# Mixture-of-experts stage of an attention kernel: expert tiles of 128 slots instead of 256, three weight sets with guarded loads, and tiles past the 36th in conditional blocks

## The chip, the cores and the metric

The kernel runs on one core of one Trainium2 chip. The metric is device time in microseconds (us); lower is better. The engines are named as the profile names them: PE (TensorE, matmuls) with PEld (its weight loads), DVE (VectorE), ACT (ScalarE), POOL (GpSimd) and SP (SyncE, which here only issues DMAs).

## What is computed

Two stages in one program, all in float32. First a sliding-window causal attention (8 batches, 8 heads, 576 positions, head size 64, window 64). Its output, laid out as 4608 tokens of 512 numbers, feeds a mixture of experts in which every token goes to exactly one of 8 experts.

```python
scores = np.where((rel >= 0) & (rel < 64), q @ k.T / 8, -1e9)
attn = softmax(scores); x = (attn @ v) as (4608, 512)
logits = x @ w_gate                      # (4608, 8)
expert_idx = np.argmax(logits, axis=1)
gate_w = softmax(logits)[arange, expert_idx]
for e in range(8):                       # rows of x grouped by expert
    h = np.maximum(x_sorted[lo:hi] @ w1[e], 0.0)   # w1[e]: 512 x 1024
    y_sorted[lo:hi] = h @ w2[e]                    # w2[e]: 1024 x 512
out = gate_w[:, None] * y_in_token_order
```

The inputs are drawn with a fixed seed. With them the experts 0 to 7 get 669, 400, 748, 505, 592, 390, 566 and 738 tokens.

## The kernel before

The program has three stages.

Attention: for each of 8 batches and 4 head pairs the kernel transposes q and k on PE, makes the scores of three blocks of 64 queries at a time, adds a mask, exponentiates, and multiplies by v. Every two batches it makes the router logits (line 234, matmuls with 8 columns) and writes x to memory (`x_dram`). SP loads q, k and v of a batch while the one before is at work, in two sets of buffers.

Routing: the kernel ranks every token within its expert and gives it a slot. Slots are cut into tiles of TB = 256, each tile belonging to one expert; an expert's last tile may be partly empty. `tile_e` holds the expert of each tile. From the slots two tables are made by one-hot matmuls (`lo`, `hi`, `slots`, lines 385 to 400): `perm_i`, the token of each slot, and `gate_s`, its gate.

Experts (lines 428 to 470): there are NTILE = 18 + 7 = 25 tiles, enough for any routing, and all 25 are computed. `fetch(i)` has SP load both weight matrices of the tile's expert, 2 MB each, into one of two sets (`wp`, bufs=2), whatever the tile before used, and has POOL gather the 256 tokens by an indirect DMA in two halves of 128 rows (`xg`). For each tile PE then does

- 8 transposes of the gathered rows (line 437), copied to `xgT` by DVE and ACT,
- the first product `hp`, 8 groups of 4 matmuls with 256 columns (line 445), each group made positive and copied to `hT` by DVE or ACT,
- the second product `yp`, 2 halves of 8 matmuls with 512 columns (line 456), scaled by the gate and scattered to the output by an indirect DMA of POOL.

A float32 matmul that is not a transpose is two PE instructions, each with a weight load of its own, so a tile has 64 of the first kind and 32 of the second. A scheduler orders each engine's instructions by a model of their cost; buffers in pools make the waits.

```python
fetched = {0: fetch(0)}
for i in range(NTILE):
    if i + 1 < NTILE:
        fetched[i + 1] = fetch(i + 1)
    w1, w2, xg = fetched.pop(i)
```

Of the kernel before, what the change touches and what calls it, by code (L numbers as in the profile page):

```python
# [18 lines left out]
WINDOW = 64  # L19
# [15 lines left out]
def kernel(  # L35
# [18 lines left out]
    NG = H // 2              # head pairs: one pair fills the 128 partitions  # L54
    NB = S // WINDOW         # query blocks of one window; each sees itself and the block before
    GB = 3                   # query blocks handled together
    KB = (S + P - 1) // P    # row tiles of 128, the last one half full
    NV = NB // 2             # whole ones
    SM = NV * P
    BG = 2                   # batches that together fill whole token blocks  # L60
    NTB = BG * S // P        # token blocks in such a group
    NJ = NT // P             # token blocks in all
    FT = FF // P
    TB = 256                 # slots of one expert tile
    C = TB // P
    NTILE = (NT + TB - 1) // TB + E - 1   # enough for any routing
    NS = NTILE * C
# [7 lines left out]
    # x in token order, and after it one row of zeros for the slots without a token  # L75
# [8 lines left out]
    tile_e = consts.tile([P, NTILE], I32, name="tile_e")  # L84
    zrow = consts.tile([1, DM], F32, name="zrow")
    nc.vector.memset(zrow[:], 0.0)

# [1 line left out]
    with (  # L89
# [12 lines left out]
        # additive masks over [(head, query), key]: slot 0 for the first block, whose  # L102
        # keys are blocks 0 and 1; the others for the keys of the block before and its own
# [17 lines left out]
        # q transposed, each head of the pair in its own columns and zeros beside it  # L121
# [19 lines left out]
        def load_v(b):  # L141
# [5 lines left out]
            # the same keys half a tile later  # L147
# [137 lines left out]
    with (  # L285
# [12 lines left out]
        e_m = iota([P, E], [[1, E]], base=-E)                    # e - E  # L298
# [4 lines left out]
        tok_m = iota([P, NJ], [[P, NJ]], base=-NT, cm=1)         # token - NT, never 0  # L303
        before = rt.tile([P, P], F32, name="before")             # [p', p] = p' < p
# [6 lines left out]
        keep = rt.tile([P, E, NJ], F32, name="keep")             # 0 where a scan starts again  # L311
# [7 lines left out]
        # the first expert of the largest logit, and its probability  # L319
# [16 lines left out]
        # rank of a token among those of its expert: lower partitions of its column, columns before  # L336
# [14 lines left out]
        # tiles of each expert, up to and with it, and the slot where it starts  # L351
# [17 lines left out]
        V.tensor_copy(out=tile_e[:], in_=te[:])  # L369

# [13 lines left out]
        # the other way round: token and gate of every slot [slot % P, slot // P]  # L384
# [18 lines left out]
    w1v = moe_w1.rearrange("e (g p) f -> p e g f", p=P)  # L403
    w2v = moe_w2.rearrange("e (t p) d -> p e t d", p=P)
    with (
        tc.tile_pool(name="wp", bufs=2) as wp,
        tc.tile_pool(name="mp", bufs=2) as mp,
# [91 lines left out]
```

## Time and profile before

| | us |
|---|---|
| three runs | 1118.69, 1118.84, 1123.08 (median 1118.84) |
| span of the profiled execution | 1121.2 |
| attention, up to the last router logits | 333.8 |
| routing and first gathers | 51.4 |
| 25 expert tiles, first `hp` to last `yp` | 724.9 |
| after the last matmul | 11.1 |

| engine | busy us | share of the span |
|---|---|---|
| PE | 1031.5 | 92% |
| PEld | 753.1 | 67% |
| DVE | 350.9 | 31% |
| ACT | 277.1 | 25% |
| POOL | 211.8 | 19% |

The profile records one execution, with every instruction's start and duration by engine and by line, the DMA traffic, and the TensorE clock that was granted (1.00 is 2.4 GHz, 0.50 is 1.2 GHz). Times are counted from the span's start. Matmuls are pipelined: the duration of one is longer than the distance between two starts, so the cost of a stream of matmuls is read from starts. A row that says x20 merges 20 instructions that follow each other.

### The profile page before, as it was taken

The numbers are of one execution on the slowest core, as the hardware profiler recorded it, in microseconds if no ns is written. First come the engines' busy times: TensorE is split into PE (matmuls) and PEld (weight loads), VectorE is DVE, ScalarE is ACT, GpSimd is POOL, SyncE is SP. The second block draws the span as 40 slices with busy tenths as digits, with TensorE's granted clock in tenths as the row PEclk, the third lists the DMA queues.
The fourth block names the chain that finished last, engine by engine and source line by source line (L and its number), as shares of the span: only waits on it lengthen the run. The fifth ranks groups of instructions, "written<-read, shape, count | busy, mean of one in ns | idle before, by whom it ended". The sixth has DMA issues, their size and how long they took to land. (4 is left out here: it accounts for less than half of the span.)

```text
span 1121.2 us, 13320 instructions
## 1 busy us (share of the span) xinstructions
PE 1031.5 (92%) x4868; PEld 753.1 (67%) x4868; DVE 350.9 (31%) x949; ACT 277.1 (25%) x968; POOL 211.8 (19%) x243
## 2 busy tenths in 40 slices
PE   5999898988975699999999999999999999999996
PEld 4888887877864566666666666666666666666663
DVE  5887787877847010111111011111101111111010
ACT  3675675765730000100000000000000000000000
POOL 3442342333220400111111111111111111110000
PEclk9999999999975799999999999999999999999998
DMA  9873654762002774444444555554544445454400
GB/s 198 142 127 109 140 92 133 123 124 89 1 1 85 284 266 176 175 165 170 165 179 178 184 188 187 188 182 170 188 174 170 169 159 174 182 185 150 150 1 0
DMA packets 165491, 166.04 MB, mean 148 GB/s; under 512 B 116912, under 2 KB 116912, under 8 KB 165426
## 3 DMA queue, kind: packets, MB, share of 16 engines
q1 hardware_dynamic: 152242, 133.20, 40.9%
q0 software_dynamic: 8000, 22.56, 5.3%
q10 hardware_dynamic: 5184, 9.44, 2.2%
q8 instruction: 38, 0.62, 0.2%
q14 instruction: 27, 0.22, 0.1%
HBM read 146.29 MB, written 22.55 MB: 151 GB/s over the span
## 5 line engine op out<-in xcount | busy, mean ns | idle before, releaser
L445 PE MATMUL hp<-xgT,w 128*128 128x256 f32 x1600 | 352.3, 381 | 0.8 <-ACT xgT L438 0.8
L456 PE MATMUL yp<-w,hT 128*128 128x512 f32 x800 | 347.4, 592 | 0.0
L445 PEld LDWEIGHTS hp<-xgT,w 128*128 128x128 f32 x1600 | 303.1, 191 | 43.3 <-ACT xgT L438 1.0
L456 PEld LDWEIGHTS yp<-w,hT 128*128 128x128 f32 x800 | 152.0, 190 | 180.7 <-issue 179.4
L467 POOL DMA_INDIRECT out_dram<-y,perm_i x50 | 50.0, 1001 | 532.9 <-DVE y L465 492.1
L452 DVE TENSOR_SCALAR hT<-hp 128x256 f32<-128x256 f32 x100 | 42.5, 425 | 302.6 <-PE hp L445 302.6
L450 ACT ACTIVATE hT<-hp 128x256 f32<-128x256 f32 x100 | 38.4, 384 | 326.3 <-PE hp L445 245.3
L204 POOL TENSOR_TENSOR pr<-pr,sm 128x384 f32<-128x384 f32 x96 | 79.4, 828 | 206.2 <-DVE sm L203 68.9
L198 ACT ACTIVATE pr<-pr,mx 128x128 f32<-128x128 f32 x288 | 112.6, 392 | 21.5 <-DVE mx L195 18.7
L463 ACT ACTIVATE y<-yp,gate_s 128x512 f32<-128x512 f32 x25 | 17.2, 688 | 334.4 <-PE yp L456 334.4
L186 PE MATMUL sc<-kT,qd 128*128 128x128 f32 x576 | 90.5, 287 | 2.5 <-DVE pr L192 1.3
L465 DVE TENSOR_SCALAR y<-yp,gate_s 128x512 f32<-128x512 f32 x25 | 18.8, 751 | 202.2 <-PE yp L456 202.2
L186 PEld LDWEIGHTS sc<-kT,qd 128*128 128x128 f32 x576 | 75.8, 196 | 7.0 <-DVE pr L192 3.9
L421 POOL DMA_INDIRECT xg<-x_dram,perm_i x50 | 49.3, 986 | 157.2 <-PE tp L437 100.2
L210 PE MATMUL pt<-ident,pr 128*128 128x128 f32 x288 | 54.5, 292 | 19.1 <-POOL pr L204 17.5
L438 DVE COPY xgT<-tp 128x512 f32<-128x512 f32 x25 | 17.3, 692 | 150.7 <-PE tp L437 149.3
L217 PE MATMUL pv<-pT,va 128*128 128x128 f32 x320 | 61.4, 291 | 3.0 <-DVE pT L212 2.7
L192 DVE TENSOR_TENSOR pr<-sc,mask 128x384 f32<-128x384 f32 x96 | 52.7, 549 | 17.0 <-PE sc L186 14.8
L212 DVE COPY pT<-pt 128x384 f32<-128x384 f32 x96 | 52.6, 550 | 17.1 <-PE pt L210 16.2
L210 PEld LDWEIGHTS pt<-ident,pr 128*128 128x128 f32 x288 | 33.7, 147 | 30.4 <-POOL pr L204 29.4
L198 ACT ACTIVATION_READ_ACCUMULATOR pr<-pr,mx 128x1 f32 x288 | 53.9, 187 | 0.0
L217 PE MATMUL pv<-pT,vb 128*128 128x128 f32 x256 | 52.3, 288 | 0.6 <-ACT xT L224 0.3
(94 smaller groups left out, 760.7 us busy)
## 6 DMA issues: line engine op xcount, KB each, us to landing
w<-in_moe_w_dram SPq DMA_DIRECT2D x50, 2048.0 KB, 9.4
x_dram<-xs ACTq DMA_DIRECT2D x36, 256.0 KB, 2.0
qs<-in_q_dram SPq DMA_DIRECT2D x32, 256.0 KB, 5.0
ks<-in_k_dram SPq DMA_DIRECT2D x32, 256.0 KB, 5.1
va<-in_v_dram SPq DMA_DIRECT2D x32, 256.0 KB, 5.0
qs<-in_q_dram SPq DMA_DIRECT2D x8, 128.0 KB, 5.0
ks<-in_k_dram SPq DMA_DIRECT2D x8, 128.0 KB, 4.6
vb<-in_v_dram SPq DMA_DIRECT2D x8, 128.0 KB, 4.5
```

Of the source, the lines that this page charges most:

```text
L186: nc.tensor.matmul(sc[:, n, :], lhsT=qd[:, i].rearrange("d h s -> d (h s)"), rhs=kT[:, k0 : k0 + P], start=True, stop=True,)
L192: nc.vector.tensor_tensor(out=pr[:], in0=sc[:], in1=mask[:, m0 : m0 + GB, :], op=ALU.add)
L198: nc.scalar.activation(out=pr[:, n, :], in_=pr[:, n, :], func=AF.Exp, scale=scale, bias=mx[:, n : n + 1], accum_out=sm[:, n : n + 1],)
L204: nc.gpsimd.tensor_tensor(out=pr[:], in0=pr[:], in1=_inner(sm[:], P), op=ALU.mult)
L210: nc.tensor.transpose(out=pt[:, n, :], in_=pr[:, n, :], identity=ident[:])
L212: nc.vector.tensor_copy(out=pT[:], in_=pt[:])
L217: nc.tensor.matmul(pv[:, n, :], lhsT=vt[:, 2 * g : 2 * g + 2, :].rearrange("p h d -> p (h d)"), rhs=pT[:, n, :], start=True, stop=True,)
L421: nc.gpsimd.indirect_dma_start(out=t[:], out_offset=None, in_=x_dram[:, :], in_offset=bass.IndirectOffsetOnAxis(ap=perm_i[:, i * C + c : i ...
L445: nc.tensor.matmul(hp[:], lhsT=w1[:, 0, g, f * P : (f + 1) * P], rhs=xgT[:, g, :], start=(g == 0), stop=(g == NG - 1),)
L452: nc.vector.tensor_scalar_max(hT[:, f, :], hp[:], 0.0)
L456: nc.tensor.matmul(yp[:], lhsT=hT[:, f, c * P : (c + 1) * P], rhs=w2[:, 0, f, :], start=(f == 0), stop=(f == FT - 1),)
L467: nc.gpsimd.indirect_dma_start(out=out[:, :], out_offset=bass.IndirectOffsetOnAxis(ap=perm_i[:, s : s + 1], axis=0), in_=y[:], in_offset=N ...
```

## The change

A tile holds 128 slots. The most tiles any routing can need is now 36 + 7 = 43. With the token counts above, the experts need 6, 4, 6, 4, 5, 4, 5 and 6 tiles, 40 in all.

- A tile has one gather, 4 transposes (`turn`), a first product of 32 matmuls with 128 columns in two groups of 16 that each fill one PSUM tile and are copied by one instruction (DVE for the first, ACT for the second), a second product of 8 matmuls with 512 columns, one scaling on ACT and one scatter. The transposes of tile i+1 stand in the code between the two products of tile i.
- Tile i uses weight set i mod 3. `load_i` says for each tile whether its expert differs from that of the tile three before; the two weight DMAs of a tile are issued with that as a condition. Set 0 is filled with expert 0's weights during the attention stage (after the loads of the last batch in the code), and tile 0 reloads it only where its expert is not 0. Gathered rows have four buffers. SP keeps the order of the code in the expert stage.
- Tiles 0 to 35 always run. Every engine then reads the number of used tiles (`used`), and tiles 36 and up stand in four blocks of two (the last of one), each under a condition.
- In the routing stage the tables have 43 instead of 50 columns, the cuts 36 instead of 18, and `used_i` and `load_i` are made.

```diff
-    TB = 256                 # slots of one expert tile
-    C = TB // P
-    NTILE = (NT + TB - 1) // TB + E - 1   # enough for any routing
-    NS = NTILE * C
+    TB = P
+    NTILE = (NT + TB - 1) // TB + E - 1
+    NS = NTILE
+    NW = 3
...
+    load_i = consts.tile([P, NTILE], I32, name="load_i")
+    used_i = consts.tile([P, 1], I32, name="used_i")
...
+    ws = [weights(consts, 0)]
...
+                if b + 2 == B:
+                    nc.sync.dma_start(out=ws[0][0][:], in_=w1v[:, 0:1, :, :])
+                    nc.sync.dma_start(out=ws[0][1][:], in_=w2v[:, 0:1, :, :])
...
+        V.tensor_copy(out=used_i[:], in_=cum[:, E - 1 : E])
+
+        V.tensor_single_scalar(load_i[:, 0:1], te[:, 0:1], 0.0, op=ALU.not_equal)
+        V.memset(load_i[:, 1:NW], 1)
+        V.tensor_tensor(out=load_i[:, NW:], in0=te[:, NW:], in1=te[:, 0 : NTILE - NW], op=ALU.not_equal)
...
-        tc.tile_pool(name="wp", bufs=2) as wp,
+        tc.tile_pool(name="wp", bufs=1) as wp,
...
-        tc.tile_pool(name="ps_h", bufs=3, space=PSUM) as ps_h,
+        tc.tile_pool(name="ps_h", bufs=4, space=PSUM) as ps_h,
         tc.tile_pool(name="ps_y", bufs=2, space=PSUM) as ps_y,
+        tc.manual_schedule(engines={mybir.EngineType.SP}),
...
+        def fetch(i):
+            w1, w2 = ws[i % NW]
             e = nc.sync.value_load(tile_e[0:1, i : i + 1], min_val=0, max_val=E - 1)
...
+            new = nc.sync.value_load(load_i[0:1, i : i + 1], min_val=0, max_val=1)
+            nc.sync.dma_start(out=w1[:], in_=w1v[:, bass.ds(e, 1), :, :], cond=new, cond_hint=False)
+            nc.sync.dma_start(out=w2[:], in_=w2v[:, bass.ds(e, 1), :, :], cond=new, cond_hint=False)
+            nc.gpsimd.indirect_dma_start(
+                out=xgs[i % NX][:], out_offset=None, in_=x_dram[:, :],
+                in_offset=bass.IndirectOffsetOnAxis(ap=perm_i[:, i : i + 1], axis=0),
+            )
+
+        def turn(i):
+            tp = ps_xt.tile([P, NG, P], F32, name="tp")
+            for g in range(NG):
+                nc.tensor.transpose(out=tp[:, g, :], in_=xgs[i % NX][:, g * P : (g + 1) * P], identity=ident[:])
+            nc.vector.tensor_copy(out=xgTs[i % 2][:], in_=tp[:])
+
+        def work(i, ahead):
...
+            for m in range(2):
+                hp = ps_h.tile([P, HF, TB], F32, name="hp")
+                for f in range(HF):
+                    for g in range(NG):
+                        c0 = (m * HF + f) * P
+                        nc.tensor.matmul(
+                            hp[:, f, :], lhsT=w1[:, 0, g, c0 : c0 + P], rhs=xgT[:, g, :],
+                            start=(g == 0), stop=(g == NG - 1),
+                        )
+                if m:
+                    nc.scalar.activation(out=hT[:, m * HF :, :], in_=hp[:], func=AF.Relu)
+                else:
+                    nc.vector.tensor_scalar_max(hT[:, 0:HF, :], hp[:], 0.0)
+            if ahead:
+                turn(i + 1)
...
+        for i in range(NCUT):
+            fetch(i + AHEAD)
+            work(i, True)
+
+        used = nc.values_load(used_i[0:1, 0:1], min_val=NCUT, max_val=NTILE)
+        for i0 in range(NCUT, NTILE, 2):
+            with tc.If(used > i0):
+                for i in range(i0, min(i0 + 2, NTILE)):
+                    if i + AHEAD < NTILE:
+                        fetch(i + AHEAD)
+                    work(i, i + 1 < NTILE)
```

Below are the instructions as the built programs have them; xK means K equal rows, and one row of a float32 matmul is two PE instructions on the chip. PE in the middle of the expert stage, before (`xg`: gathered rows, `tp`: transposes, `hp`: first product, `yp`: second):

```order
L445 MATMUL hp<-xgT,w_4486 128x256 x32
L456 MATMUL yp<-w_4488,hT 128x512 x16
L437 MATMUL tp<-ident,xg_4597 128x128
L437 MATMUL tp<-ident,xg_4599 128x128 x4
L437 MATMUL tp<-ident,xg_4704 128x128 x3
L445 MATMUL hp<-xgT,w_4593 128x256 x32
```

The same place of the changed program:

```order
L460 MATMUL hp<-xgT_4270,w_0_73 128x128 x32
L448 MATMUL tp<-ident,xg_4265 128x128 x4
L472 MATMUL yp<-w_0_74,hT 128x512 x8
L460 MATMUL hp<-xgT_4269,w_1_4261 128x128 x32
L448 MATMUL tp<-ident,xg_4266 128x128 x4
L472 MATMUL yp<-w_1_4262,hT 128x512 x8
```

The transposes, which stood between one tile's second product and the next tile's first, now stand between the two products of a tile and are for the tile after.

SP in the expert stage, two tiles of before (each DMA is one weight matrix of 2 MB; ISA rows set registers; the experts' numbers were all read earlier):

```order
L415 ISA
L415 DMA w_5021<-in_moe_w_dram 128x4x1024
L417 ISA
L417 DMA w_5023<-in_moe_w_dram 128x8x512
L415 ISA
L415 DMA w_5128<-in_moe_w_dram 128x4x1024
L417 ISA
L417 DMA w_5130<-in_moe_w_dram 128x8x512
```

One tile of the changed program:

```order
L436 TENSOR_LOAD tile_e
L436 ISA x2
L437 TENSOR_LOAD load_i
L437 ISA x2
L438 ISA
L438 DMA w_0_73<-in_moe_w_dram 128x4x1024
L439 ISA
L439 DMA w_0_74<-in_moe_w_dram 128x8x512
```

SP now reads the expert and the condition of each tile just ahead of its two loads. In the attention stage the scheduler has put the load of set 0's first matrix between the loads of v for batch 3 and those of q for batch 4, and the second between those for batches 5 and 6.

PE at the end of the program, before:

```order
L445 MATMUL hp<-xgT,w_6626 128x256 x32
L456 MATMUL yp<-w_6628,hT 128x512 x16
L437 MATMUL tp<-ident,xg_6737 128x128
L437 MATMUL tp<-ident,xg_6739 128x128 x4
L445 MATMUL hp<-xgT,w_6733 128x256 x32
L456 MATMUL yp<-w_6735,hT 128x512 x16
L494 UNCONDITIONAL_BRANCH
```

PE of the changed program around tile 36:

```order
L448 MATMUL tp<-ident,xg_4265 128x128 x4
L472 MATMUL yp<-w_2_4264,hT 128x512 x8
L491 TENSOR_LOAD used_i
L493 COMPARE_AND_BRANCH
L460 MATMUL hp<-xgT_4269,w_0_73 128x128 x32
L448 MATMUL tp<-ident,xg_4266 128x128 x4
L472 MATMUL yp<-w_0_74,hT 128x512 x8
L460 MATMUL hp<-xgT_4270,w_1_4261 128x128 x32
L448 MATMUL tp<-ident,xg_4267 128x128 x4
L472 MATMUL yp<-w_1_4262,hT 128x512 x8
L493 UNCONDITIONAL_BRANCH x2
L493 COMPARE_AND_BRANCH
```

Each engine reads `used` once after tile 35 and then compares and branches on its own at each block; there is no barrier between the engines there. A block that is skipped has a short path of its own in which the engine raises its semaphores by what the block would have.

## Rows read from the trace of the kernel before

**Rows 1.** The page: PE's busy time, and the granted clock in 40 slices.

```profile
PE 1031.5 (92%) x4868; PEld 753.1 (67%) x4868; DVE 350.9 (31%) x949; ACT 277.1 (25%) x968; POOL 211.8 (19%) x243
...
PEclk9999999999975799999999999999999999999998
```

**Rows 2.** Windows by stage: start:end, length, busy us by engine, PEclk, DMA share, GB/s.

```profile
0.00:333.80 333.80, 287.44 (x2156) 255.37 (x2156) 248.57 (x759) 206.59 (x813) 112.47 (x143) 0.96 0.54 107
...
385.20:1110.10 724.90, 715.78 (x2578) 475.23 (x2576) 77.18 (x148) 65.98 (x147) 88.11 (x89) 1.00 0.48 169
1110.10:1121.20 11.10, 0.00 (x0) 0.00 (x0) 0.00 (x0) 0.69 (x1) 0.98 (x1) 0.71 0.00 0
```

**Rows 3.** The page's costliest groups: busy us, mean ns | idle before, releaser.

```profile
L445 PE MATMUL hp<-xgT,w 128*128 128x256 f32 x1600 | 352.3, 381 | 0.8 <-ACT xgT L438 0.8
L456 PE MATMUL yp<-w,hT 128*128 128x512 f32 x800 | 347.4, 592 | 0.0
L445 PEld LDWEIGHTS hp<-xgT,w 128*128 128x128 f32 x1600 | 303.1, 191 | 43.3 <-ACT xgT L438 1.0 <-issue 1.0
```

**Rows 4.** Timeline of PE, one expert tile: start us, length us, instruction.

```profile
1022.58 0.71 PE L437 MATMUL tp<-ident,xg 128*128 128x128 f32 x5
1023.69 0.55 PE L437 MATMUL tp<-ident,xg 128*128 128x128 f32 x3 [0.40 <-DVE xgT L438]
1024.07 14.05 PE L445 MATMUL hp<-xgT,w 128*128 128x256 f32 x64
1037.96 13.90 PE L456 MATMUL yp<-w,hT 128*128 128x512 f32 x32
1051.69 0.71 PE L437 MATMUL tp<-ident,xg 128*128 128x128 f32 x5
```

**Rows 5.** Timeline of PE in the attention stage: matmuls with 128 and with 8 columns.

```profile
201.65 0.83 PE L186 MATMUL sc<-kT,qd 128*128 128x128 f32 x6
...
84.94 1.73 PE L234 MATMUL xo<-wg,xT 128*128 128x8 f32 x14
```

**Rows 6.** Line 186 by itself: durations in ns, least/median/most.

```profile
L186 PE MATMUL sc<-kT,qd x576: 274/275/580, 13.9 to 316.2; 128*128 128x128 f32 x192
L186 PEldq EVENT_SEMAPHORE  x5: 51/51/51, 33.8 to 274.9; - x5
```

**Rows 7.** Timeline from the end of the routing to the first expert tile.

```profile
359.24 10.43 PE L395 MATMUL slots<-hi,lo 128*128 128x100 f32 x72 [3.64 <-DVE hi L392]
...
378.33 5.48 PE L437 MATMUL tp<-ident,xg 128*128 128x128 f32 x20 [8.67 <-issue]
379.61 0.69 DVE L438 COPY xgT<-tp 128x512 f32<-128x512 f32 x1 [9.58 <-PE tp L437]
...
385.27 15.16 PE L445 MATMUL hp<-xgT,w 128*128 128x256 f32 x64
```

**Rows 8.** Windows over line 395 alone: PE, PEld, then PEclk, DMA share, GB/s.

```profile
363.00:364.00 1.00, 1.00 (x7) 1.00 (x7) 0.62 0.00 0
364.00:366.00 2.00, 2.00 (x20) 2.00 (x20) 1.00 0.00 0
```

**Rows 9.** The page's groups: a copy of 512 columns out of PSUM.

```profile
L465 DVE TENSOR_SCALAR y<-yp,gate_s 128x512 f32<-128x512 f32 x25 | 18.8, 751 | 202.2 <-PE yp L456 202.2
```

**Rows 10.** The page's DMA issues: KB each, median us from issue to landing.

```profile
w<-in_moe_w_dram SPq DMA_DIRECT2D x50, 2048.0 KB, 9.4
```

**Rows 11.** Windows at the start of the expert stage (columns as in rows 2).

```profile
369.00:379.00 10.00, 1.33 (x9) 1.19 (x9) 0.33 (x2) 0.00 (x0) 5.92 (x6) 0.75 0.81 291
379.00:392.00 13.00, 12.34 (x48) 9.56 (x48) 1.97 (x4) 1.56 (x3) 5.69 (x6) 0.67 1.02 374
```

**Rows 12.** Timeline of SP: the last load for batch 3, the first for batch 4.

```profile
106.57 0.61 SPq L146 DMA_DIRECT2D vb<-in_v_dram  x1
119.77 0.37 SPq L136 DMA_DIRECT2D qs<-in_q_dram  x1
```

**Rows 13.** Groups of DVE in the routing stage: one of three on the table `hi`.

```profile
L392 DVE TENSOR_TENSOR hi<-hi,iota 128x1800 f32<-128x1800 f32 x1 | 2.0, 2026 | 0.0
```

**Rows 14.** Timeline of POOL after the last matmul.

```profile
1111.14 0.98 POOL L467 DMA_INDIRECT out_dram<-y,perm_i  x1 [5.86 <-ACT y L463]
```

More of the change, by code (lines that the diff above doesn't have):

```diff
@@ L84 @@
     tile_e = consts.tile([P, NTILE], I32, name="tile_e")
+    load_i = consts.tile([P, NTILE], I32, name="load_i")
+    used_i = consts.tile([P, 1], I32, name="used_i")
+    w1v = moe_w1.rearrange("e (g p) f -> p e g f", p=P)
+    w2v = moe_w2.rearrange("e (t p) d -> p e t d", p=P)
+    weights = lambda pool, i: [
+        pool.tile([P, 1, NG, FF], F32, name=f"w1_{i}"), pool.tile([P, 1, FT, DM], F32, name=f"w2_{i}")
+    ]
+    ws = [weights(consts, 0)]
     zrow = consts.tile([1, DM], F32, name="zrow")
@@ L400 @@
         V.tensor_copy(out=gate_s[:], in_=slots[:, 1, :])
-    w1v = moe_w1.rearrange("e (g p) f -> p e g f", p=P)
-    w2v = moe_w2.rearrange("e (t p) d -> p e t d", p=P)
     with (
-        tc.tile_pool(name="wp", bufs=2) as wp,
+        tc.tile_pool(name="wp", bufs=1) as wp,
         tc.tile_pool(name="mp", bufs=2) as mp,
+        tc.tile_pool(name="xgp", bufs=1) as xgp,
         tc.tile_pool(name="ps_xt", bufs=2, space=PSUM) as ps_xt,
-        tc.tile_pool(name="ps_h", bufs=3, space=PSUM) as ps_h,
+        tc.tile_pool(name="ps_h", bufs=4, space=PSUM) as ps_h,
@@ L410 @@
         tc.tile_pool(name="ps_y", bufs=2, space=PSUM) as ps_y,
+        tc.manual_schedule(engines={mybir.EngineType.SP}),
     ):
+        HF = FT // 2
+        NX = 4
+        ws += [weights(wp, i) for i in range(1, NW)]
+        xgs = [xgp.tile([P, DM], F32, name=f"xg{i}") for i in range(NX)]
+        xgTs = [xgp.tile([P, NG, TB], F32, name=f"xgT{i}") for i in range(2)]
         def fetch(i):
+            w1, w2 = ws[i % NW]
             e = nc.sync.value_load(tile_e[0:1, i : i + 1], min_val=0, max_val=E - 1)
-            w1 = wp.tile([P, 1, NG, FF], F32, name="w1")
@@ L415, in fetch @@
-            nc.sync.dma_start(out=w1[:], in_=w1v[:, bass.ds(e, 1), :, :])
-            w2 = wp.tile([P, 1, FT, DM], F32, name="w2")
-            nc.sync.dma_start(out=w2[:], in_=w2v[:, bass.ds(e, 1), :, :])
-            xg = []
-            for c in range(C):
-                t = mp.tile([P, DM], F32, name=f"xg{c}", bufs=3)
-                nc.gpsimd.indirect_dma_start(
-                    out=t[:], out_offset=None, in_=x_dram[:, :],
-                    in_offset=bass.IndirectOffsetOnAxis(ap=perm_i[:, i * C + c : i * C + c + 1], axis=0),
-                )
-                xg.append(t)
@@ new lines, in turn @@
+        def turn(i):
[4 more added lines that the diff above has]
+        def work(i, ahead):
+            w1, w2 = ws[i % NW]
+            xgT = xgTs[i % 2]
+            hT = mp.tile([P, FT, TB], F32, name="hT")
+            for m in range(2):
[13 more added lines that the diff above has]
+                turn(i + 1)
+            yp = ps_y.tile([P, DM], F32, name="yp")
+            for f in range(FT):
+                nc.tensor.matmul(
+                    yp[:], lhsT=hT[:, f, :], rhs=w2[:, 0, f, :], start=(f == 0), stop=(f == FT - 1),
+                )
+            y = mp.tile([P, DM], F32, name="y", bufs=4)
+            nc.scalar.activation(out=y[:], in_=yp[:], func=AF.Copy, scale=gate_s[:, i : i + 1])
+            nc.gpsimd.indirect_dma_start(
+                out=out[:, :], out_offset=bass.IndirectOffsetOnAxis(ap=perm_i[:, i : i + 1], axis=0),
+                in_=y[:], in_offset=None, bounds_check=NT - 1, oob_is_err=False,
+            )
@@ new lines @@
+        AHEAD = NW - 1
+        for i in range(AHEAD):
+            fetch(i)
+        turn(0)
+        for i in range(NCUT):
[8 more added lines that the diff above has]
+                    work(i, i + 1 < NTILE)
```

43 lines of the change are left out of this document (removed).

## Prediction

> **What bounds the kernel now.** I read the page first: PE is busy 92% of the span, no other engine over 31%, at a granted clock of 9 tenths or more except around slices 13 and 14 [rows 1]. The windows by stage show where that lies: in the 724.9 us of the expert stage PE is busy 715.8 us at the full clock, while DVE, ACT and POOL are each busy about a tenth of it and the DMA engines half of it [rows 2]. So this stage is as long as its matmuls, and only fewer or shorter PE instructions can shorten it. Attention is different: PE is idle 46 of its 333.8 us [rows 2]. The change barely touches it.
>
> Next comes the price of a matmul, from starts. In a tile the 64 instructions of the first product start at 1024.07 and the second product at 1037.96: 0.217 us each for 256 columns. The 32 of the second run to 1051.69: 0.429 us for 512. The eight transposes with a wait of 0.40 us for DVE's copy take 1.49 us. The period is 29.1 us [rows 4]; 25 of them are the stage. The groups confirm it: the sum of the busy times is 352.3 and 347.4 us [rows 3].
>
> **What the change does to the work.** Before, 25 tiles of 256 are computed whatever the routing, 6400 slots for 4608 tokens. By the token counts (each divided by 128, rounded up) the experts need 40 tiles of 128, that is 5120 slots. 36 run always; blocks 36-37 and 38-39 run, the last two are skipped. Columns through PE fall by a fifth if a matmul of 128 columns costs half of one of 256. Whether it does is the main question, because each still needs its own weight load.
>
> **First product with 128 columns.** Rows of the same form exist in attention. Six score matmuls of 128 columns take 0.83 us [rows 5], of which the last one's own 0.275 [rows 6] is latency: five starts in 0.555, 0.111 us each. Fourteen router matmuls with only 8 columns take 1.73 us [rows 5], at most 0.124 each, and about 0.113 with a tail like the other's taken off. So the weight load, not the columns, sets some 0.112 us, and at 128 columns the load and the columns are nearly equal. The bounds are 0.108 (half of 0.217) and 0.124. I take 0.112, nearest to the score row, since it is the same shape: 64 x 0.112 = 7.17 us.
>
> The Trainium skill speaks against small tiles: "Perfetto Trace Analysis", Optimizing Tensor Performance, says larger matmuls are more efficient, and "TensorE: Matmul & The Clock Gate", Back-to-back issue gap, has sustained spacings of 81 ns at 128 columns and 131 at 512, a ratio of 0.62. By that ratio an instruction of 128 columns would be 0.62 x 0.429 = 0.265 us and the time would be that of the second rival below. The trace's ratio is 0.112 to 0.429, or 0.26.
>
> **Rest of a tile.** Second product: 16 x 0.429 = 6.86 us, as before per slot. Four transposes: the first five of a group take 0.71 us and the last one's tail overlaps, so 0.11 each, 0.44 us. The wait of 0.40 us goes: one PSUM tile per `turn`, two buffers, the gathered rows fetched two tiles ahead. A PE semaphore instruction is 51 ns [rows 6]; a tile has up to three, which may hide behind queued matmuls; I take one, 0.06 us, with ends 0 and 0.15. A tile is then 7.17 + 6.86 + 0.44 + 0.06 = 14.53 us, with ends 14.2 and 15.4.
>
> What hides the rest: the copy of a 512-column PSUM tile takes 0.75 us [rows 9]. DVE's copy of the first half of `hp` lies under the second half (3.6 us). ACT's copy of the second half lies under the transposes and the first eight instructions of `yp` (3.4 us). The copy of `tp` lies under `yp`. DVE and ACT have two such copies in 14.5 us each, POOL one gather and one scatter of about 1 us. If a cover failed, a tile would pay about 0.8 us; I see none that does.
>
> **Weights.** 24 loads of 4 MB replace 25, so the total hardly changes, but 100 MB now move in 580 us and come in runs: a new expert loads three tiles in a row. A tile with its load, gather and scatter moves 4.7 MB. With two loads in flight the core moved 374 GB/s [rows 11]: 12.6 us, under 14.5. Also, the first matrix of a set is released by the first product of the tile three before, the second by its second product, so each load has about 36 us, against 9.4 us median for one matrix [rows 10]. SP waits in order there, but only later weight loads stand behind it; the gathers are POOL's. So: nothing. The two preloads in attention go out while SP is idle: between 106.6 and 119.8 us it has nothing to issue [rows 12], and 9.4 us fit. Cost 0. But the scheduler has ordered the instructions of the later batches differently, and PE's 46 us of idle time could grow or shrink: ends of 5 us either way.
>
> **Start of the stage.** Before, PE transposes six gathers (378.33 on) before the first product at 385.27 [rows 7]. Now two are ahead, and the first product needs only the first one's copy, which ends at 379.61 + 0.69 = 380.3. So it starts at 380.4: 4.9 us less. But the clock is low there: line 395 began at 359.24 [rows 7] at 1.2 GHz and the level rose within the microsecond from 363 [rows 8], 4.4 us later. At 1.2 GHz a matmul takes twice as long, so of 4.4 us half is lost: +2.2. In routing, three passes over `hi` of 2.03 us [rows 13] shrink by 252 of 1800 elements, -0.85; `over`, `nt`, `ended` and `te` grow by 144 each, +0.65 at the same price per element; three tiny instructions are new. Together +0.5, ends -0.5 and +2.
>
> **Conditional blocks.** The trace has no conditional branch. Three places are on PE's path: before 36, between 37 and 38, and after 39. If the next instructions are at hand and PE has queued matmuls, the cost is 0. If they must be fetched from memory, the nearest row is a DMA's landing, at most 9.4 us [rows 10], and 2.2 us more if the clock falls meanwhile. The first two fall through to code that stands next; the jump at the end of a taken block passes two instructions. So I am near the lower end: 2 us twice, +4, ends 0 and +31. Each other engine has a branch too, under PE's work. In the tail, 11.1 us pass after the last matmul [rows 2], POOL's last scatter at 1111.14 among them [rows 14]; POOL now also passes two skipped blocks: +2, ends 0 and +5.
>
> The Trainium skill, "Runtime: NRT & Kernel Launch", Instruction fetch mechanics, states that a taken branch whose target is not in the current pages stalls until a DMA has fetched it. No run here shows it yet; by that rule the first rival decides.
>
> **The sum.** Expert stage: 40 x 14.53 = 581.2, plus 2.2, against 724.9: -141.5. Start -4.9, routing +0.5, blocks +4, tail +2. Together -139.9: a span of 981.3 us. The median of the runs is 1118.84 against a span of 1121.2, a factor of 0.998: 979 us.
>
> **Rivals.**
>
> First, branches stall: three stops of 9.4 us, each with a lower clock after it, 35 in place of 4 us: 1010 us. For it: PE's block is over 300 instructions long. Against it: the code that runs is nearly in sequence. Chance 0.08.
>
> Second, and on the other side: the weight load doesn't overlap. The loads' own duration is 191 ns [rows 3]. Were it paid in front of each 128-column matmul, an instruction would cost 0.191 + 0.112 = 0.303 us, a tile 26.8 us, the kernel some 1470 us. By the ratio of the page of the Trainium skill it would be 0.265, a tile 24.3, the kernel some 1370. This decides from 0.168 us per instruction on (a tile of 18.1 us, 40 of which are as long as the stage now). For it: nothing has run 64 such matmuls in a row here. Against it: six score matmuls at 0.111 and fourteen at 0.12, all with their own loads. Chance 0.03.
>
> Third, the conditions don't skip: every tile loads, 4.7 MB per tile all the time. At 374 GB/s that is 12.6 us and still hidden; at the 291 GB/s of the window before it [rows 11], 16.2 us, so 40 x 16.2 = 648 and the kernel 1046 us. Chance 0.04.
>
> **How the numbers follow.** The forecast has 0.85. Its range: low, 0.108 per instruction (-10), no branch cost (-4), or attention -5, which don't add up fully: 965. High: 0.124 per instruction (+31) or branches at their upper end (+31): 1010, where the first rival lies too. A measurement of this kernel tells 0.5% from no change. Faster by more: the forecast and the first and third rivals, 0.96. Slower: the second, 0.03. Within 0.5%: 0.01 for a mixture that lands there.
>
> **What would show it.** In the profile after, the first product's 64 instructions should take 7.2 us from start to start, a tile 14.5, 36 tiles 523. PE's waits for weights should be nil in the middle of the stage. The three branch places show as gaps of PE of 0 to 3 us. The bytes on SP's queue should be 24 x 4.2 + 28 = 129 MB, not 209. The first product should start near 381, and the time behind the last matmul should be 13 us. I'd be wrong first through the 0.112 (64 x 40 times in the sum), next through a gap at each expert change, then through the branches.

## The result and the profile after

| | before | after |
|---|---|---|
| median of the runs, us | 1120.96 (1118.69 to 1123.38, 4 runs) | 992.38 (991.46 to 993.79, 4 runs) |
| span of the profiled execution, us | 1121.2 | 989.7 |

The ratio of after to before is 0.885, with a 95% interval of 0.883 to 0.8875. The forecast was 979 us, with a range of 965 to 1010.

The page of the changed kernel, PE's busy time and the granted clock in 40 slices, beside [rows 1]:

```profile
PE 900.6 (91%) x5632; PEld 710.9 (72%) x5632; DVE 330.0 (33%) x884; ACT 260.3 (26%) x898; POOL 193.9 (20%) x225
...
PEclk9999899699999755999999999999999999999997
```

PE lost 130.9 us of work, and its share of the span is nearly the same. But look at the clock in the first 14 slices, which are attention: there is now an 8 and a 6 where before stood nines. The windows by stage (columns as in [rows 2]: busy us by engine, then PEclk, DMA share, GB/s):

```profile
0.00:345.50 345.50, 293.97 (x2156) 261.71 (x2156) 250.15 (x761) 206.27 (x813) 112.39 (x143) 0.94 0.56 116
345.50:397.30 51.80, 28.41 (x120) 24.27 (x121) 24.52 (x44) 2.69 (x5) 4.84 (x5) 0.53 0.29 111
397.30:975.60 578.30, 578.27 (x3358) 424.87 (x3356) 55.32 (x80) 50.70 (x79) 75.64 (x77) 1.00 0.57 197
975.60:989.70 14.10, 0.00 (x0) 0.00 (x0) 0.00 (x0) 0.69 (x1) 1.00 (x1) 0.61 0.05 15
```

The expert stage is 578.2 us instead of 724.8, and PE is busy in all of it. Attention ends at 345.5 instead of 333.8 us, though its PE instructions are the same in kind and number (2156 in both): PE is busy 293.97 us with them instead of 287.44 (6.5 more) and idle 51.5 us instead of 46.4 (5.2 more).

The groups of PE in the expert stage (columns as in [rows 3]), where no group has any idle time before it:

```profile
L460 PE MATMUL hp<-xgT,w 128*128 128x128 f32 x2560 | 292.8, 275 | 0.0
L472 PE MATMUL yp<-w,hT 128*128 128x512 f32 x640 | 281.3, 592 | 0.0
```

One tile on PE's timeline, beside [rows 4]:

```profile
455.21 7.31 PE L460 MATMUL hp<-xgT,w 128*128 128x128 f32 x64
462.35 0.60 PE L448 MATMUL tp<-ident,xg 128*128 128x128 f32 x4
462.79 7.03 PE L472 MATMUL yp<-w,hT 128*128 128x512 f32 x16
469.66 1.05 PE L460 MATMUL hp<-xgT,w 128*128 128x128 f32 x8
```

From start to start: 64 matmuls of 128 columns in 7.14 us (0.1116 each), four transposes in 0.44, sixteen of 512 columns in 6.87 (0.429 each), together 14.45. From the first tile to the second it is 14.53 us, and each of the other 38 distances between tiles is 14.45, at every change of expert too.

The time behind the slots' matmuls came out as forecast, but the time of these matmuls themselves didn't. Timeline of PE, beside [rows 7]:

```profile
371.00 15.66 PE L411 MATMUL slots<-hi,lo 128*128 128x86 f32 x72 [8.38 <-DVE hi L408]
```

Before, the run took 10.43 us. The difference of the spans, place by place (attention is taken to the start of its last copy of logits):

| place | before, us | after, us | difference | forecast |
|---|---|---|---|---|
| attention, to the last copy of logits | 333.82 | 345.49 | +11.7 | 0 |
| from there to the slots' matmuls | 25.42 | 25.51 | +0.1 | +0.5 |
| slots' matmuls | 10.43 | 15.66 | +5.2 | not in the sum |
| from there to the first product | 15.61 | 10.67 | -4.9 | -4.9 |
| expert stage with its blocks | 724.82 | 578.24 | -146.6 | -137.5 |
| after the last matmul | 11.1 | 14.1 | +3.0 | +2 |
| span | 1121.2 | 989.7 | -131.5 | -139.9 |

So the span came out 8.4 us over the forecast's 981.3 by misses of opposite sign: 17 us that it didn't see ahead of the expert stage, and 9 us that it charged to the stage and that weren't paid. The other 5 of the 13 us between 979 and 992.38 come from the step from span to time. The forecast multiplied by 0.998, the median of the runs before over the span of one profiled execution, but that execution was slower than the median: in every run whose span is on record the time is 1.7 to 2.0 us longer than the span, so a span of 1121.2 belongs to a run of some 1123 us. The experiments ask what caused the 17 us.

### The profile page after: what moved, and what is told of

Read it like the earlier page. It is cut to its first block, busy times and chain, and to the rows that moved or that the text cites. A ratio compares the mean times of both kernels' runs of the same rounds, so it can differ in the third digit from the quotient of the medians.

```text
span 989.7 us, 15089 instructions
## 1 busy us (share of the span) xinstructions
PE 900.6 (91%) x5632; PEld 710.9 (72%) x5632; DVE 330.0 (33%) x884; ACT 260.3 (26%) x898; POOL 193.9 (20%) x225
## 3 DMA queue, kind: packets, MB, share of 16 engines
q1 hardware_dynamic: 150674, 129.00, 45.4%
## 5 line engine op out<-in xcount | busy, mean ns | idle before, releaser
L460 PEld LDWEIGHTS hp<-xgT,w 128*128 128x128 f32 x2560 | 292.7, 192 | 18.7 <-issue 18.7
L460 PE MATMUL hp<-xgT,w 128*128 128x128 f32 x2560 | 292.8, 275 | 0.0
L472 PE MATMUL yp<-w,hT 128*128 128x512 f32 x640 | 281.3, 592 | 0.0
L472 PEld LDWEIGHTS yp<-w,hT 128*128 128x128 f32 x640 | 118.5, 190 | 133.9 <-issue 133.9
L467 DVE TENSOR_SCALAR hT<-hp 128x512 f32<-128x512 f32 x40 | 27.7, 692 | 389.4 <-PE hp L460 389.4
L478 POOL DMA_INDIRECT out_dram<-y,perm_i x40 | 40.5, 1013 | 315.2 <-ACT y L476 301.8
L465 ACT ACTIVATE hT<-hp 128x512 f32<-128x512 f32 x40 | 23.9, 598 | 297.4 <-PE hp L460 297.4
L476 ACT ACTIVATE y<-yp,gate_s 128x512 f32<-128x512 f32 x40 | 27.5, 687 | 266.1 <-PE yp L472 266.1
L449 DVE COPY xgT<-tp 128x512 f32<-128x512 f32 x41 | 28.3, 691 | 137.0 <-PE tp L448 137.0
L220 DVE COPY pT<-pt 128x384 f32<-128x384 f32 x96 | 52.7, 550 | 16.6 <-PE pt L218 15.8
L225 PEld LDWEIGHTS pv<-pT,va 128*128 128x128 f32 x320 | 49.0, 203 | 6.1 <-DVE pT L220 4.6
```

What stands on the lines that cost most here:

```text
L220: nc.vector.tensor_copy(out=pT[:], in_=pt[:])
L225: nc.tensor.matmul(pv[:, n, :], lhsT=vt[:, 2 * g : 2 * g + 2, :].rearrange("p h d -> p (h d)"), rhs=pT[:, n, :], start=True, stop=True,)
L449: nc.vector.tensor_copy(out=xgTs[i % 2][:], in_=tp[:])
L460: nc.tensor.matmul(hp[:, f, :], lhsT=w1[:, 0, g, c0 : c0 + P], rhs=xgT[:, g, :], start=(g == 0), stop=(g == NG - 1),)
L472: nc.tensor.matmul(yp[:], lhsT=hT[:, f, :], rhs=w2[:, 0, f, :], start=(f == 0), stop=(f == FT - 1),)
L478: nc.gpsimd.indirect_dma_start(out=out[:, :], out_offset=bass.IndirectOffsetOnAxis(ap=perm_i[:, i : i + 1], axis=0), in_=y[:], in_offset=N ...
```

## The experiments

**Attention's 11.7 us: the preloads.** My theory was that the two preloads of set 0 (4.2 MB) cost it; what stayed open was whether by their traffic or because the scheduler orders the instructions of attention differently when they are there. Without them the order on PE and ACT is instruction for instruction that of the kernel before.

```
-                if b + 2 == B:
-                    nc.sync.dma_start(out=ws[0][0][:], in_=w1v[:, 0:1, :, :])
-                    nc.sync.dma_start(out=ws[0][1][:], in_=w2v[:, 0:1, :, :])
...
-        V.tensor_single_scalar(load_i[:, 0:1], te[:, 0:1], 0.0, op=ALU.not_equal)
-        V.memset(load_i[:, 1:NW], 1)
+        V.memset(load_i[:, 0:NW], 1)
```

> The changed kernel without its two preloads: tile 0 loads set 0 inside the expert stage, like every other tile; set 0 is not in the memory that the routing uses, so its load can start at about 360 us and is needed at 397. The order of attention's instructions is again that of the kernel before. Attention ended 11.7 us later after the change (last logits copy at 345.5 instead of 333.8 us). If the preloads are the cause, by their traffic or by the other order that they bring: last logits copy at 333.8, span 989.7 - 11.7 = 978.0 us. If something else in the changed kernel delays attention: 345.5 and 989.7 us. If the load of set 0 is not hidden in the stage, the first product starts later than 10.7 us after the slots' matmuls, by up to 10 us, and the gain is lost there.

Measured: 979.61 us (977.92 to 983.09, 6 runs), span 976.8, ratio to before 0.8745 [0.8718, 0.8772]. The last copy of logits, on DVE's timeline:

```profile
329.68 0.23 DVE L245 COPY logits<-xo 128x72 f32<-128x72 f32 x1 [2.74 <-PE xo L242]
```

And SP's timeline, where tile 0's load is issued:

```profile
343.55 0.40 SPq L434 DMA_DIRECT2D w<-in_moe_w_dram  x1
344.23 0.39 SPq L435 DMA_DIRECT2D w<-in_moe_w_dram  x1
```

The preloads are the cause, and they bought little: without them set 0 is asked for at 343.55 and first used at 384.14, 10.6 us behind the slots' matmuls, as with them. But its load now runs beside the last writes of x, and in the routing DVE waits for one of these writes:

```profile
351.84 0.69 DVE L254 COPY xs<-xo 128x512 f32<-128x512 f32 x1 [2.17 <-DMA x_dram<-xs]
```

Of the seven profiles, here and below, in which the changed kernel loads set 0 behind attention, five have such a wait (2.15 to 2.51 us); of the four with full preloads none has. So in this profile attention gave back 15.8 us and the routing took 2.7 of them.

Attention even ended 4 us sooner than in the kernel before, which has the same order. That is the scatter of this stage: in five executions in this order without any preload the last copy began at 333.82, 329.68, 330.80, 331.47 and 329.66 us. In four in the changed kernel's order with full preloads it began at 345.49, 342.67, 347.48 and 342.55. The means are 331.1 and 344.5, a difference of 13.5 us.

**Traffic or order?** The size of the preloads decides which order the scheduler makes, so preloads of two sizes part the two. C is 512 and then 384 of 1024 columns:

```
-                    nc.sync.dma_start(out=ws[0][0][:], in_=w1v[:, 0:1, :, :])
-                    nc.sync.dma_start(out=ws[0][1][:], in_=w2v[:, 0:1, :, :])
+                    nc.sync.dma_start(out=ws[0][0][:, :, :, 0:C], in_=w1v[:, 0:1, :, 0:C])
+                    nc.sync.dma_start(out=ws[0][1][:, :, :, 0:C // 2], in_=w2v[:, 0:1, :, 0:C // 2])
```

> Both preloads cut to half of their columns (2.1 MB instead of 4.2; tile 0 then loads set 0 in full in the stage). The order of PE's and ACT's instructions in attention is that of the changed kernel. If the order costs the 11.7 us: last logits copy at 345.5, span 990 us. If the traffic costs it, in proportion to its bytes: 339.6 and 984 us.

> Both preloads cut to 3/8 of their columns (1.6 MB; tile 0 loads set 0 in full in the stage). At this size the order of PE's, DVE's and ACT's instructions in attention is that of the kernel before, at nearly the traffic of the run with half of the columns. If the order costs the 11.7 us: last logits copy at 333.8, span 978 us. If the traffic costs it, in proportion to its bytes: 338.2 and 982.4 us.

Measured: with half, in the changed kernel's order, 993.28 us (992.31 to 995.23), attention's end at 346.72; with 3/8, in the order of before, 982.00 us (980.39 to 984.62), end at 335.07. Half of the traffic brings back nothing of the whole time, and with the other order attention ends 11.6 us sooner. These two still differ by a third in their bytes, so I took the pair on either side of the size at which the order switches, 432 and 448 columns:

> Both preloads cut to 432 of 1024 columns (1.77 MB; tile 0 loads set 0 in full in the stage). This is just below the size at which the scheduler switches: the order of attention is still that of the kernel before. If the order costs most of the 11.7 us: last logits copy at 333 to 336 us, span 981 to 984. If the traffic costs it, in proportion to its bytes: 335 + 0.5 us in addition to what 3/8 of the columns showed, and the same as with 448 columns.

> Both preloads cut to 448 of 1024 columns (1.84 MB, 4% more than with 432). Now the order of attention is that of the changed kernel but for a few places. If the order costs most of the 11.7 us: last logits copy at 343 to 347 us, span 990 to 994, some 10 us more than with 432 columns. If the traffic costs it: within 1 us of the run with 432 columns, where executions of one kernel differ by 2 us or so.

Measured: 983.88 us (981.65 to 987.46) with 432 columns and 990.19 (985.80 to 992.55) with 448; attention ended at 335.98 and 342.71. With 4% more bytes, and another order, 6.7 us, or 6.3 between the medians of four runs each, whose ranges just touch. The windows show where the order bites. First with 432 columns, then with 448 (columns as before):

```profile
150.00:160.00 10.00, 8.78 (x69) 7.68 (x68) 9.51 (x30) 7.97 (x33) 5.31 (x6) 1.00 1.24 225
160.00:172.00 12.00, 11.68 (x99) 10.99 (x99) 9.00 (x31) 7.96 (x33) 3.31 (x4) 1.00 0.05 7
172.00:184.00 12.00, 9.80 (x83) 8.88 (x81) 9.12 (x25) 6.20 (x25) 5.04 (x5) 1.00 0.69 177
```

```profile
150.00:160.00 10.00, 7.59 (x62) 6.96 (x63) 9.63 (x24) 6.65 (x28) 5.83 (x5) 1.00 1.16 202
160.00:172.00 12.00, 11.51 (x94) 10.62 (x93) 9.44 (x33) 8.12 (x37) 3.31 (x4) 1.00 0.23 31
172.00:184.00 12.00, 11.74 (x60) 11.21 (x60) 5.99 (x19) 4.18 (x17) 2.82 (x4) 0.57 0.56 109
```

PE's timeline with 448 columns has the idle time of the first window in one piece:

```profile
154.49 0.29 PE L242 MATMUL xo<-wg,xT 128*128 128x8 f32 x2
157.16 0.49 PE L225 MATMUL pv<-pT,vb 128*128 128x128 f32 x2 [2.38 <-DVE pT L220]
```

In this order PE stands for 2.4 us at a `pv` whose `pT` DVE hasn't copied yet; the changed kernel has the same wait, 2.37 us at 157.68. In the order of before the scores and other `pv` come in between, and no such wait stands there. Some 15 us later the granted clock is at 0.57 for 12 us: PE is busy 11.74 of 12 us and issues 60 instructions, where with 432 columns it issues 83 in 9.80. The changed kernel shows the same 0.57 and 60 in these 12 us. The fall comes with the order: over the 25 us from 160 to 185 the granted clock is 0.78 to 0.80 in all six profiles in the changed kernel's order (or nearly that order, with 448 columns), and 0.93 to 1.00 in all seven in the order of before. Here the changed kernel, and then the run without preloads, with nearly the same number of matmuls:

```profile
160.00:185.00 25.00, 24.49 (x164) 23.03 (x163) 16.40 (x55) 13.09 (x55) 5.88 (x8) 0.80 0.45 86
```

```profile
160.00:185.00 25.00, 21.22 (x165) 19.41 (x164) 17.98 (x52) 13.81 (x55) 9.14 (x9) 0.93 0.39 103
```

That the wait brings about the fall is not shown, and the trace speaks against it: between the two PE works 11.51 of 12 us at the full clock. What stands shortly ahead of the fall, in the changed kernel, is a run of 16 matmuls with 8 columns:

```profile
170.04 1.95 PE L242 MATMUL xo<-wg,xT 128*128 128x8 f32 x16
```

```profile
170.00:172.00 2.00, 2.00 (x19) 1.95 (x17) 1.48 (x5) 1.26 (x6) 0.83 (x1) 1.00 0.02 4
172.00:174.00 2.00, 1.97 (x12) 1.41 (x12) 0.88 (x3) 0.31 (x1) 0.30 (x1) 0.78 0.00 0
174.00:178.00 4.00, 4.00 (x19) 3.86 (x19) 2.25 (x8) 2.12 (x8) 0.52 (x1) 0.50 0.02 4
```

The order of before has such a run too (at 162.62 without preloads). Which part of the order holds the clock down for longer no run takes apart.

The traffic has a share of its own. Waits of PE between 105 and 125 us, where the first preload is on its way (engine, line, what it waits for, us in total, times, longest), with 432 columns and then without a preload:

```profile
PE xo L242 <- DVE xs L254: 3.2, 1, 3.2
PE pt L218 <- POOL pr L212: 2.1, 4, 0.8
```

```profile
PE pt L218 <- POOL pr L212: 2.8, 4, 1.6
PE xo L242 <- DVE xs L254: 0.4, 1, 0.4
```

`xs` is what ACT's queue writes to `x_dram`; with the preload beside it (289 GB/s instead of 161 from 105 to 115 us) DVE waits 2.7 us for an earlier write to land before it can copy into `xs` again, and PE waits for its PSUM tile:

```profile
116.83 0.69 DVE L254 COPY xs<-xo 128x512 f32<-128x512 f32 x1 [2.69 <-DMA x_dram<-xs]
```

The changed kernel has one such wait of PE of 3.5 us there and one of 3.6 us at 191, in its second preload. Its copies into `xs` wait 10.6 us in all for such landings in the first 340 us:

```profile
ACT xs L254 <- DMA x_dram<-xs: 6.5, 2, 5.7
DVE xs L254 <- DMA x_dram<-xs: 4.1, 2, 3.6
```

In the five profiles without preloads it is 1.1 to 2.2 us.

How much is traffic and how much order is read best from PE's busy and idle time up to the last copy of logits, in all 13 profiles, each with the same 2156 instructions:

| preloads | order of PE's instructions | profiles | PE busy, us | PE idle, us |
|---|---|---|---|---|
| none | before | 5 | 282.5 to 287.4 | 46.2 to 47.3 |
| 1.6 and 1.8 MB | before | 2 | 285.9 and 286.2 | 49.2 and 49.8 |
| 1.8 and 2.1 MB | changed (1.8 MB: nearly) | 2 | 293.1 and 298.0 | 49.7 and 48.8 |
| 4.2 MB | changed | 4 | 289.8 to 296.1 | 51.4 to 52.9 |

The idle time goes with the bytes, and at 1.6 to 2.1 MB it is the same in both orders. The busy time goes with the order: the same instructions take longer at the lower clock. By the means of the first and the last row, the order has some 8 of the 13.5 us and the traffic some 5; up to 2 us of the busy time may be the traffic's too (the second row against the mean of the first, 284.2). No run has the full preloads in the order of before, so this split is read from the table and not from one run.

**The slots' matmuls.** NS is the number of columns of both tables:

```
-    NS = NTILE
+    NS = 50
```

> The changed kernel with tables of 50 columns instead of 43, so that the 36 slots matmuls have 100 columns, as in the kernel before, instead of 86 (the last seven columns stay unused). Attention and its order are as in the changed kernel. Theory: with 86 columns the granted clock stays at its lower level for the whole run of these matmuls (15.7 us), with 100 it rises after 4.4 us as before (10.4 us). Then -5.2 us for the matmuls and +0.8 for the passes over hi: span 985.3 us. Rival: the clock stays low because of when the run comes, not how long its matmuls are: the matmuls take 15.7 us or a little longer, span 990.5 us.

Measured: 988.86 us (984.88 to 992.03), span 983.2; its median is 3.5 us below the changed kernel's, and the profiled run is the fastest of its four, so the gain is read from the matmuls themselves. Timeline, and below it the windows of the first 6 us with the clock (PE, PEld and the other engines, then PEclk):

```profile
369.40 10.11 PE L411 MATMUL slots<-hi,lo 128*128 128x100 f32 x72 [9.17 <-DVE hi L408]
```

```profile
369.40:371.40 2.00, 2.00 (x9) 2.00 (x10) 0.00 (x0) 0.00 (x0) 0.00 (x0) 0.50 0.00 0
371.40:373.40 2.00, 2.00 (x12) 2.00 (x11) 0.00 (x0) 0.00 (x0) 0.00 (x0) 0.54 0.04 8
373.40:375.40 2.00, 2.00 (x20) 2.00 (x20) 0.00 (x0) 0.00 (x0) 0.00 (x0) 1.00 0.00 0
```

In the changed kernel the granted clock stays at 0.50 (1.2 GHz) in every window from 371 to 387. In all nine profiles with 84 or 86 columns the run took these 15.66 us, wherever it began between 355.9 and 374.8 us, and in none of the four with 100 (10.43, 10.11, 11.15 and 10.15 us), which began between 357.2 and 369.4. So it isn't a matter of when the run comes, nor of how long PE stood idle before it (2.74 to 10.99 us in the nine, 3.64 to 11.46 in the four). Why the narrower run stays at the low clock is open. The kernel before with 21 tiles, below, has 84 columns and shows 15.66 too: the narrower table alone does it. Of the 6.5 us by which this span is shorter, the slots' matmuls have 5.6; attention ended 2.8 us sooner by its scatter, the tail was 0.5 shorter, and the way to these matmuls, with the passes over the wider `hi` (1.2), and a first tile that began at the low clock (15.82 us instead of 14.53) gave back 2.5.

**Both together.** No preloads and NS = 50:

> No preloads and tables of 50 columns together. If the preloads delay attention by 11.7 us and the 86 columns keep the clock low for 5.2 us: 989.7 - 11.7 - 5.2 + 0.8 = 973.6 us of span, last logits copy at 333.8, slots matmuls in 10.4 us. If either is wrong, 978 or 985 us. If the rise of the clock is a matter of when the run comes, it could go either way here too, independent of the 100 columns.

Measured: 976.33 us (973.17 to 981.02, 5 runs), span 971.3, ratio to before 0.8721 [0.8696, 0.8745], attention's end at 330.80, slots in 11.15 us. The two repairs add up: against the changed kernel's 992.38 they give 16.1 us together, and 12.8 and 3.5 apart, within the runs' scatter of each other.

**The conditional blocks.**

```
-        used = nc.values_load(used_i[0:1, 0:1], min_val=NCUT, max_val=NTILE)
-        for i0 in range(NCUT, NTILE, 2):
-            with tc.If(used > i0):
-                for i in range(i0, min(i0 + 2, NTILE)):
...
+        for i in range(NCUT, 40):
```

> Exactly 40 tiles, all outside of conditional blocks, and no register read for them; it computes what this routing needs and leaves out the tiles that another routing could need. If the blocks cost only the tail (14.2 us behind the last matmul instead of 11.1): span 989.7 - 3.1 = 986.6 us, and the starts from tile to tile stay at 14.45 us. If they cost time on PE's path as I forecast (2 us at each of two borders): 982.6 us. If the tail is longer for another reason (more scatters, smaller ones): 989.7 us.

Measured: 987.67 us (986.65 to 989.34), span 987.6; the expert stage took 579.3 us, not less than with blocks, and the tail 9.4 instead of 14.1 (two gathers, for tiles 40 and 41, are left out with the blocks). On PE's path the blocks cost nothing, as the changed kernel's timeline at the border of the first one (tile 36) shows, where a tile takes 14.45 us as anywhere:

```profile
910.74 7.03 PE L472 MATMUL yp<-w,hT 128*128 128x512 f32 x16
917.61 7.31 PE L460 MATMUL hp<-xgT,w 128*128 128x128 f32 x64
924.75 0.60 PE L448 MATMUL tp<-ident,xg 128*128 128x128 f32 x4
925.19 7.03 PE L472 MATMUL yp<-w,hT 128*128 128x512 f32 x16
```

In the tail POOL passes the two skipped blocks. What stands there in the changed kernel, on the line of the blocks (durations in ns, least/median/most, first and last start):

```profile
L493 POOLq INC_SWDGE_SEM  x2: 1775/1806/1836, 976.8 to 979.8; - x2
```

The second starts at 979.8, when the last scatter has landed, and POOL's wait of some 7 us at the end of the program only behind it. With no blocks that wait begins before the last scatter is even issued. If each skipped block has its price, one fewer should help:

```
-        for i0 in range(NCUT, NTILE, 2):
+        cut = [NCUT, NCUT + 2, NCUT + 4, NTILE]
+        for i0, i1 in zip(cut, cut[1:]):
```

> The kernel without preloads and with tables of 50 columns, and the last two conditional blocks (tiles 40 and 41, tile 42) merged into one, so that this routing skips one block instead of two. In the changed kernel POOL passes two long increments of DMA semaphores in the skipped blocks (1.84 and 1.78 us), the second of which starts when the last scatter has landed, and its last wait of some 7 us starts only behind them; with all 40 tiles outside of blocks the time behind the last matmul was 9.4 us, with two skipped blocks 14.0. If each skipped block costs its share: 1.8 to 3 us less, 11 to 12.2 us behind the last matmul, span 968.5 to 969.5 us. If one increment that waits for the last scatter's landing is enough to hold POOL up: 14 us, and no change. The stage stays at 578.5 us either way.

Measured: 974.24 us (973.95 to 980.17, 5 runs), ratio to before 0.870 [0.8676, 0.8723], span 972.3, tail 13.55 us. The expected gain of 1.8 to 3 us in the tail was 0.4: the rival holds. The one increment that is left waits for the last scatter in the same way:

```profile
L490 POOLq INC_SWDGE_SEM  x1: 1835/1835/1835, 962.5 to 962.5; - x1
```

It is the fastest kernel here by its median, but 974.24 and 976.33 can't be told apart by their runs.

**Do the skipped loads matter?**

```
-        V.tensor_tensor(out=load_i[:, NW:], in0=te[:, NW:], in1=te[:, 0 : NTILE - NW], op=ALU.not_equal)
+        V.memset(load_i[:, NW:], 1)
```

> Every tile from the third on loads its weights, whether the expert changes or not: 40 loads and more of 4.2 MB, 1.0 to 1.1 GB/ms. At the 374 GB/s that two loads in flight reached, a load with its gather and scatter takes 12.6 us and stays hidden under a tile of 14.45 us: about 990 us, so that skipping the loads is worth nothing. At 291 GB/s it takes 16.2 us: the tiles run at the pace of the loads, about 1060 us, and the conditions are needed for the gain.

Measured: 990.82 us (989.37 to 992.26), span 987.7. The queue of SP (packets, MB, share), in the changed kernel and then here, with the expert stage's window here behind it:

```profile
q1 hardware_dynamic: 150674, 129.00, 45.4%
```

```profile
q1 hardware_dynamic: 178898, 204.50, 66.8%
```

```profile
400.00:970.00 570.00, 570.00 (x3313) 418.86 (x3313) 54.24 (x79) 50.68 (x79) 74.75 (x75) 1.00 0.92 329
```

The rate in the expectation's first sentence is wrong (42 loads of 4.2 MB in 578 us are 0.3 GB/ms); its sum goes by 374 and 291 GB/s and stands. With 75 MB more, PE still never waits. The loads run at 329 GB/s all the time, with the DMA engines at a share of 0.92, and fit just under the tiles. For the time the conditions on the loads are worth nothing here.

**Fewer tiles or smaller ones?** Of the kernel before:

```
-    NTILE = (NT + TB - 1) // TB + E - 1
+    NTILE = 21
```

> The kernel before with 21 tiles of 256 slots instead of 25: it leaves out the tiles that are empty for this routing. 4 x 29.1 = 116.4 us less than its 1121: about 1004.6 us. It tells apart the two halves of the gain: tiles that needn't be computed, and smaller tiles with fewer empty slots (40 x 14.45 = 578 us instead of 21 x 29.1 = 611). If the empty tiles were cheaper than the full ones, the gain would be less.

Measured: 1008.88 us (1008.38 to 1009.38), ratio to before 0.900 [0.8973, 0.9028], span 1006.7. Its expert stage:

```profile
387.60:996.90 609.30, 601.80 (x2162) 399.47 (x2160) 64.60 (x124) 55.18 (x123) 71.70 (x72) 1.00 0.48 170
```

Of the 146.6 us that the stage gained, 115.5 come from not computing the four tiles that are empty, and 31.1 from smaller tiles with fewer empty slots and without a wait in them.

## Why the prediction was right, and where it missed

The mechanism of the main term was right. That the time lay in the range owes something to luck. The range reached up to 1010 for dearer matmuls and for branches, which didn't come; the 17 us ahead of the expert stage, which the sum didn't see, used that room, and 9 us of costs that weren't paid made up for half of them.

- **The matmul of 128 columns** at 0.112 us was right (0.1116), and with it the main term. The five starts between six score matmuls [rows 5, 6] had shown it. The rival by the ratio of the Trainium skill ("TensorE: Matmul & The Clock Gate", Back-to-back issue gap: 81 to 131 ns, 0.62) fell: the ratio here is 0.1116 to 0.429, or 0.26, over 2560 and 640 instructions.
- **A tile** was forecast at 14.53 and took 14.45. The 0.06 us for a semaphore in each tile weren't paid; with the rounding of 0.112 that is 3 us over 40 tiles.
- **The low clock at the start of the stage**, +2.2, is real, but its size depends on the moment: the first tile took 14.53 us after the change, so 0.1, and 14.59 to 16.14 in the other runs of 40 tiles (0.1 to 1.7 us).
- **The blocks on PE's path**, +4, cost 0. "Runtime: NRT & Kernel Launch" of the Trainium skill, Instruction fetch mechanics, has a stall where a taken branch leaves the instructions at hand; the trace shows no gap on PE at the blocks that run, so the first rival fell. PE enters these blocks by falling through, and the jump at their end passes two instructions, so no run here shows such a stall or rules it out.
- **The weights** were right: no wait of PE, 129.00 MB on SP's queue, so the premise of the third rival (no skipping) was false. Even with it the time would have been that of the forecast: loading always costs nothing, since 329 GB/s are sustained where I had put 291 as the lower rate.
- **The start** (-4.9) and the routing's DVE work (+0.1 for +0.5) were right. The slots' matmuls I left out of the sum altogether: I counted the narrower tables as a gain of 0.85 us on DVE and didn't ask what they change on PE, though [rows 7, 8] held the low clock and its rise in that very run. That is 5.2 us.
- **The step that failed** is "Cost 0" for the preloads, with "ends of 5 us either way" for the other order: 11.7 us. I judged the transfers by whether SP's queue was idle, but beside them the writes of x from ACT's queue land later, and PE is idle longer (5.2 us more in this profile). And I put the other order down as a shift of PE's idle time, where its price is PE's own work at a lower clock (6.5 us more busy time for the same 2156 instructions). Together they are over the 5 us that I gave as the end.
- **The tail**, +2, was +3.0, for the reason given (skipped blocks on POOL). The price of the blocks is 4.7: without them the tail is 9.4, where the kernel before has 11.1, and 9.8 with 21 tiles.
- **Slips in the sums.** The factor 0.998 took 2 us off the span, where a run's time is 1.7 to 2.0 us longer than its own span. Thirteen starts in 1.73 less 0.275 us are 0.112 each and not 0.113, and the chances of the forecast and of the first and third rivals add up to 0.97 and not 0.96; these two change nothing.

## What to carry to other kernels

Price a smaller matmul from starts of the same shape in the trace, not from columns, and count empty tiles first: four fifths of the stage's gain came from not computing them. A transfer moved to a place where its queue is idle was not free here: other writes landed later beside it, and the scheduler changed the order of the other work. Its normal place was already 40 us ahead of its use and cost some 2 us of the routing in most profiles, where the preloads cost 13. Compare the instruction order of every stage that the edit doesn't mean to touch, and look at the granted clock there before calling it unchanged.

## What the runs showed of the hardware

- 36 matmuls of 86 or 84 columns, 72 instructions back to back, ran at a granted clock of 0.50 from beginning to end, 0.2175 us each and 15.66 us in all, in nine profiles; with 100 columns the clock rose to 1.00 some 4 to 6 us into the run, in four. The narrower table made the run some 5 us longer.
- PE took float32 matmuls of 128 columns, each with its own weight load, at 0.1116 us each, 64 in a row, and worked for 578 us without a gap, also at conditional blocks whose code is run.
- A skipped block has a price on POOL, where it increments the semaphores of the DMAs left out: 1.8 us each, the last of them behind the landing of the last scatter, with the end of the program behind it. The tail is 4.7 us longer with two such blocks, and 4.1 with one (13.55 against 9.4).
- 329 GB/s of loads, gathers and scatters ran beside 570 us of unbroken matmuls, with no wait on PE.
- Loads of 4.2 MB beside attention left PE idle some 5 us longer, and of 1.6 to 2.1 MB some 2.5 us, in either order of its instructions: copies waited until writes of x had landed (9.3 to 10.6 us in all beside 4.2 MB, 1.1 to 2.2 without), and PE waited for the copies.
- Another order of the same 2156 PE instructions made PE's busy time some 8 us longer, with a granted clock of 0.78 to 0.80 instead of 0.93 to 1.00 from 160 to 185 us.
